# A linear-attention and maxout kernel: nine tokens per partition for k and v, 64-row pairs on TensorE, and q's maxima applied to the numerators

## The chip, the cores and the metric

The kernel runs on one core of one Trainium2 chip. A core has five engines that are used here: TensorE (PE, its weight loads are shown apart as PEld), VectorE (DVE), ScalarE (ACT), GpSimd (POOL) and SyncE (SP), which issues most of the transfers. Times are device microseconds (us) of the whole program; lower is better. The kernel before takes 297.06 us, the median of three runs (296.61 to 297.08).

## The reference

Sixty-four attention heads (8 batches of 8), 576 tokens each, 64 channels. Each head is a linear attention with a feature map phi, and what comes out goes through a feed-forward layer with a maximum over three projections:

```python
def phi(x):                                   # x: q or k, (b, h, 576, 64)
    proj = einsum('bhsd,df->bhsf', x, w_phi)  # 128 features
    proj = proj - max(abs(proj), axis=-1, keepdims=True)
    return concatenate([exp(proj), exp(-proj)], axis=-1)
q_p, k_p = phi(q), phi(k)
kv  = einsum('bhsf,bhsd->bhfd', k_p, v)       # sum over tokens
z   = sum(k_p, axis=2)
num = einsum('bhsf,bhfd->bhsd', q_p, kv)
den = einsum('bhsf,bhf->bhs', q_p, z)[..., None] + 1e-06
x   = num / den                               # to (4608, 512)
h   = maximum(maximum(x @ w1, x @ w2), x @ w3)
out = h @ w_out
```

With m the row maximum and p the projection, the first half of phi is exp(p - m) and the second exp(-(p - m)), so a token's factor is exp(-m) on the one and exp(m) on the other. For k both factors can be put on v. For q a common factor of both halves cancels in num / den, and what is left is exp(-2m) on the first half alone.

## The kernel before

**Tiling.** A unit is 4 heads of one batch; 16 units make the 64 heads, units 2b and 2b+1 make batch b. A unit's 4 × 576 tokens stand in 18 tiles of 128 tokens: 16 "main" tiles (4 per head, a partition holds 4 consecutive tokens of a head) and 2 tail tiles (the last 64 tokens of two heads each, one head in partitions 0 to 63, the other in 64 to 127). The same layout holds for q, k and v, so each of them is loaded by one main transfer (rows of 1,024 bytes) and two tail transfers (rows of 256 bytes).

**One unit's steps** (function `attention`):
- T: q and k are turned into `qkT` (q's channels in rows 0 to 63, k's in rows 64 to 127), by 36 TensorE transposes for units 0 to 3 (line 517), by a transfer that transposes (line 530) for the others.
- G: projections of both with `w2` into PSUM tiles `psq` and `psk`: per main tile two matmuls that use 64 rows each (line 557), per tail tile one of 128 rows and 256 columns (line 552).
- Ek: two exponentials of each group of k's projections on ACT (line 570); maxima of |projection| for q and k on DVE (line 576).
- em, vab, vtl: the factors exp(-m), exp(m) of k (line 613), times v on POOL (lines 618 and 633).
- M: q's projections again, with features on partitions, minus q's maxima. For units 0 to 3 the maxima are subtracted by further matmuls with `minus`, the negated identity (lines 655 and 657: 18 products of 128 columns per unit). For the others the maxima are transposed (pmT, line 584), copied (line 588) and put by a transfer (line 592) into row 64 of `qkT`, which k's channels no longer need, and one matmul with `wphi_m` (row 64 holds -1) does both (line 653).
- Eq: two exponentials of each group (line 665).
- K: key features times values, 18 matmuls of 128 rows per pair of heads (lines 682 and 685), copied to `kv_sb` (line 689).
- N: numerators and denominators, 10 matmuls of 65 columns per head into one PSUM tile (line 703); DVE takes a reciprocal and multiplies (lines 709 and 710) into `x_sb`.
- X: `x_sb` transposed into `xT`, on TensorE and a copy (lines 723 and 726) for units 0 to 5, by a transfer (line 733) for the others.

**Feed-forward.** Function `chunk` runs nine times: for each batch its tokens 0 to 511, and last for the 64 tail tokens of all 8 batches (512 again). It does 54 + 54 up projections in all, each of 4 matmuls of 512 columns (line 756), the maxima (lines 762, 764, 766), and the down projections (lines 784 and 789), copied out (line 797) and stored. Before the first chunk, differences of the weights (line 831), a transposed w1 (lines 843 and 846) and its product with w_out (lines 857 and 861) are made.

**Order.** Nothing is scheduled at run time. The string `PLAN` is an order table written out by hand or by a planner: 1,542 words, each a node's number, its engine, the slots of its buffers and a planned start. `plan` sorts nothing: the nodes are emitted in the order of the words, and each engine executes its own in that order, waiting by semaphores for what it needs. All PSUM tiles share 8 banks. `fill` adds matmuls on a constant tile `idle` (line 889, called idlers) where the table leaves TensorE free for long, from the planned end of the node that sets `idle` (node 2, `2D0@0.5`) on.

## Time and profile before

| what | value |
|---|---|
| median of three runs | 297.06 us (296.61 to 297.08) |
| span of the profiled execution, first to last instruction | 295.1 us |
| mean granted TensorE clock in it | 0.998 |
| DVE busy | 214.3 us (73%) |
| ACT busy | 196.3 us (67%) |
| POOL busy | 138.1 us (47%) |
| instructions on PE | 2,973 matmuls, 3,015 weight loads |

The profile gives no device time of the profiled execution beside its span; the span is 1.96 us (297.06 - 295.1) shorter than the median of the runs, which is what lies around it (launch and end).

How to read it: a row of groups gives line, engine, operation, output<-input, shape, count, then busy time, mean ns of one, idle time before and what ended it. A row of the timeline gives start and length in us, then engine and operation. Matmuls are pipelined, so a matmul's length (about 380 ns for 512 columns) is longer than the distance to the next one (about 216 ns); costs on a busy engine are therefore read as distances from start to start. A row of windows gives a stretch, its length, and for each engine the busy time in it with the number of instructions, then the granted clock, the busy share of the transfers' engines and GB/s.

### The profile page before, as it was taken

To read this page: it belongs to the slowest core of one execution; us is meant where nothing else is said; L and a number is where in the kernel's file an instruction comes from. 1 tells how busy PE (TensorE), PEld (TensorE's weight loads), DVE (VectorE), ACT (ScalarE), POOL (GpSimd) and SP (SyncE) were. 2 spreads that over 40 slices of the span, in tenths; PEclk is the share of its full clock that TensorE was granted. 3 is DMA by queue.
4 is the path that set the end of the run, shared out by engine and by line. 5 is a ranking of instruction groups with operands and counts; after the bars stand their busy time and mean duration, and the time that the engine had idled before them with its cause. 6 is when DMAs were issued, how large, how long until landed. Compare 5 with 4: busy or idle time off the path is not lost.

```text
span 295.1 us, 7535 instructions
## 1 busy us (share of the span) xinstructions
PE 281.6 (95%) x2973; PEld 161.5 (55%) x3015; DVE 214.3 (73%) x453; ACT 196.3 (67%) x457; POOL 138.1 (47%) x172
## 2 busy tenths in 40 slices
PE   8699999999999999999999999999999999999994
PEld 3356676556556556556556555655555564444442
DVE  5793798987878988888879776889697365061541
ACT  2499888587878599979879788867954870300300
POOL 4487995672773464943982369009072500000000
PEclk9999999999999999999999999999999999999999
DMA  6999998799379979997979779935392034300306
GB/s 134 190 196 224 229 221 286 167 234 226 99 182 328 209 203 318 230 230 167 285 165 189 220 204 244 189 102 117 90 209 64 2 83 116 142 2 0 142 8 134
DMA packets 87879, 50.02 MB, mean 170 GB/s; under 512 B 56100, under 2 KB 83364, under 8 KB 87844
## 3 DMA queue, kind: packets, MB, share of 16 engines
q1 hardware_dynamic: 81684, 44.50, 61.2%
q0 software_dynamic: 6080, 4.98, 11.0%
q8 instruction: 23, 0.38, 0.5%
q14 instruction: 12, 0.10, 0.1%
q10 hardware_dynamic: 80, 0.07, 0.1%
HBM read 34.67 MB, written 9.44 MB: 149 GB/s over the span
## 4 chain that ended last, share of the span: by engine, by line
PE 79%; DVE 9%; ACT 4%; POOL 3%; DMA 2%; issue 2%; POOLq 0%; ACTq 0%; DVEq 0%
PE ups L756 27%; PE ops L789 15%; PE ops L784 11%; PE psn L703 6%; PE kvps L682 5%; PE psq L557 4%; PE psm L653 4%; DVE mk L576 2%; DMA qk_bf<-in_q_dram 2%; ACT Ek L570 2%; DVE mqp L576 2%; DVE x_sb L710 1%; POOL vab L618 1%; PE pxT L723 1%; DVE w_bf L831 1%
## 5 line engine op out<-in xcount | busy, mean ns | idle before, releaser
L756 PE MATMUL ups<-xT,w_bf 128*128 128x512 bf16 x412 | 100.4, 379 | 2.2 <-DVE mqp L576 0.8
L665 ACT ACTIVATE Eq<-psm 128x512 bf16<-128x512 f32 (+1 forms) x160 | 79.6, 579 | 8.8 <-PE psm L653 7.3
L570 ACT ACTIVATE Ek<-psk 128x512 bf16<-128x512 f32 x128 | 70.8, 607 | 16.1 <-DVE mk L576 8.7
L618 POOL TENSOR_TENSOR vab<-v_raw,em 128x1024 bf16<-128x1024 f32 (+1 forms) x36 | 61.6, 1715 | 21.2 <-ACT em L613 20.1
L756 PEld LDWEIGHTS <-w_bf 128*128 128x128 bf16 x432 | 40.7, 98 | 45.3 <-issue 1.0
L576 DVE TENSOR_REDUCE mqp<-psq 128x4 bf16<-128x512 f32 (+1 forms) x80 | 47.7, 629 | 7.5 <-PE psk L557 4.4
L789 PE MATMUL ops<-wout_bf,hT 128*128 128x512 bf16 (+1 forms) x211 | 49.5, 373 | 0.6 <-issue 0.2
L762 DVE TENSOR_TENSOR hT<-hT,ups 128x512 bf16<-128x512 bf16 x54 | 36.0, 683 | 17.4 <-PE ups L756 9.1
L576 DVE TENSOR_REDUCE mk<-psk 128x4 f32<-128x512 f32 x64 | 42.2, 680 | 1.1 <-PE psk L557 0.7
L710 DVE TENSOR_TENSOR x_sb<-psn,rden 128x320 bf16<-128x320 f32 x64 | 31.5, 492 | 2.2
L789 PEld LDWEIGHTS <-hT 128*128 128x128 bf16 x222 | 21.1, 98 | 21.7
L797 ACT COPY osb<-ops 128x512 f32<-128x512 f32 (+1 forms) x20 | 11.5, 581 | 31.3 <-PE ops L789 23.6
L764 ACT ACTIVATE hT<-ups 128x512 bf16<-128x512 f32 x27 | 16.4, 617 | 21.5 <-PE ups L756 21.5
L703 PEld LDWEIGHTS <-Eq 128*128 128x128 bf16 x640 | 24.6, 97 | 6.8
L703 PE MATMUL psn<-kv_sb,Eq 128*128 128x65 bf16 x640 | 26.1, 194 | 0.1
L633 POOL TENSOR_TENSOR vtl<-v_raw,em 64x256 bf16<-64x256 f32 x32 | 19.7, 615 | 13.2 <-ACT em L613 10.2
L766 DVE TENSOR_SCALAR hT<-ups 128x512 bf16<-128x512 f32 x27 | 18.1, 683 | 10.6 <-PE ups L756 10.6
L784 PE MATMUL ops<-xT 128*128 128x512 bf16 x89 | 24.1, 379 | 0.4
L682 PEld LDWEIGHTS <-Ek 128*128 128x128 bf16 x512 | 21.6, 98 | 4.5 <-DVE mqp L576 0.5
L682 PE MATMUL kvps<-vab,Ek 128*128 128x65 bf16 x512 | 22.8, 194 | 0.5 <-DVE mqp L576 0.2
L504 POOL CAST qk_bf<-q_raw 128x128 bf16<-128x128 f32 (+2 forms) x22 | 16.8, 773 | 11.6 <-DMA q_raw<-in_q_dram 11.3
L797 DVE COPY osb<-ops 128x512 f32<-128x512 f32 (+1 forms) x17 | 11.4, 671 | 13.7 <-PE ops L789 13.6
(80 smaller groups left out, 333.5 us busy)
## 6 DMA issues: line engine op xcount, KB each, us to landing
v_raw<-in_v_dram SPq DMA_DIRECT2D x16, 512.0 KB, 6.8
out_dram<-osb SPq DMA_DIRECT2D x32, 256.0 KB, 2.9
k_raw<-in_k_dram SPq DMA_DIRECT2D x12, 512.0 KB, 5.6
q_raw<-in_q_dram SPq DMA_DIRECT2D x12, 512.0 KB
w_bf<-in_moe_w_dram POOLq DMA_DIRECT2D x3, 768.0 KB, 8.3
k_raw<-in_k_dram SPq DMA_DIRECT2D x16, 64.0 KB, 4.5
q_raw<-in_q_dram SPq DMA_DIRECT2D x16, 64.0 KB, 6.4
v_raw<-in_v_dram SPq DMA_DIRECT2D x16, 64.0 KB, 4.3
```

The costliest lines, as they stand in the source:

```text
L570: nc.scalar.activation(Ek[s]()[:, t0:t0 + n, :], of(1), EXP, scale=1.0 - 2.0 * s)
L576: nc.vector.tensor_reduce((mq, mk)[c]()[:, t0:t0 + n], of(c), AXX, ALU.max, apply_absolute_value=True)
L618: (nc.vector if n_.eng == "DVE" else nc.gpsimd).tensor_tensor(vab()[:, g, t0:t1, 0:D], raw_part(u, 2, t0, t1), em()[:, g, t0:t1].unsqueeze ...
L665: nc.scalar.activation(Eqb()[s][:, cols], psm()[:, 0:n * P], EXP, scale=1.0 - 2.0 * s)
L682: nc.tensor.matmul(kvps()[:, ab, g, :], lhsT=Ek[g]()[:, t, :], rhs=vab()[:, g, t, :], start=(g + ab + c == 0), stop=False)
L703: nc.tensor.matmul(psn()[:, c, :], lhsT=Eqb()[g][:, t0:t0 + P], rhs=kv()[:, pr, ab, g, :], start=(g == 0), stop=(g == 1))
L710: nc.vector.tensor_tensor(x_sb()[:, pr, :, ab, :], psn()[:, :, 0:D], rden().to_broadcast([P, 5, D]), ALU.mult)
L756: nc.tensor.matmul(ups(), lhsT=w_bf[i + 1][:, ct, j * P:(j + 1) * P], rhs=tokens_of(ct), start=(ct == 0), stop=(ct == CT - 1))
L762: nc.vector.tensor_tensor(hT()[:, j, :], hT()[:, j, :], ups(), ALU.max)
L784: nc.tensor.matmul(ops_()[:, 0:width], lhsT=tile_of(ct, tt), rhs=line_w[c_i > MOVE][:, ct, cols], start=(ct == 0), stop=False)
L789: nc.tensor.matmul(ops_()[:, 0:width], lhsT=hT()[:, j, tt * P:(tt + 1) * P], rhs=wout_bf[:, j, cols], start=False, stop=(j == JT - 1))
L797: copy_on[n_.eng](part()[:, 0:width], ops_()[:, 0:width])
```

## The change

What the changed program does otherwise:

1. **k and v: nine tokens per partition.** Two heads' 1,152 tokens are taken as one list, and each partition holds 9 consecutive ones: 64 partitions per head. One transfer (rows of 2,304 bytes) brings what three brought; k and v have no tail tiles. q keeps its layout.
2. **K as 64-row pairs.** Head ab of a pair lies in partitions 64·ab to 64·ab + 63. K is 36 matmuls of 64 rows per pair of heads, alternating between the two row halves and two PSUM tiles; units 2 to 15 do both pairs in one node. `vtl` and its instructions are gone; `vab` has 18 tiles.
3. **Transposed q as 64-row pairs.** In tiles 0 to 7 q lies in rows 0 to 63 of `qkT` and k in rows 64 to 127, in tiles 8 to 17 the other way round. M takes tiles t and t + 8 together, one in each half, with the plain weights `wph` (both halves hold w_phi). G does all 18 tiles as 64-row pairs.
4. **q's maxima on the numerators.** M no longer subtracts them: `minus`, the products of line 657, pmT, mT, the transfer of line 592, `w2`, `wphi_m`, `mqp` and their memsets are gone. N puts the two halves of phi into two PSUM tiles; ACT makes `sq` = exp(-2m) (2 small instructions per unit); DVE multiplies the first accumulator by it into `y` in SBUF, adds the second, takes one reciprocal per pair of heads, and the product with it goes to POOL (22 of 32) or DVE (10 of 32).
5. **The rest.** The copy to `xT` is 640 columns wide; POOL moves the second head's tail before it copies tails for the last chunk; `x_last` shares a slot with `q_raw`; DVE reduces k before q in each group.
6. **New order table**, 1,572 words. The node that sets `idle` is now node 1 and stands late (`1D@32.5`); the program that results has no idlers. On ACT and DVE, 36 instead of 27 of the first maxima (`hT`, a ReLU) go to ACT, and all three copies of the transposed w1.

The diff, cut to its core (`any_of` sets a node's function and lets the table choose the engine; `copy_on` is the copy of that engine):

```diff
+EARLY = 2
+PT = UT // 2
 PLAN = """
-9S0@0.7 4S@1.3 11S@2.5 13S@3.1 8S0@4.4 15S0@5.6 14S@6.9 6G0@0.5 0G@1.4 1G@2.1 7G@2.6 90G1@3.4 17G@9.3 91G@9.6 12A@6.8
...
+    def rows_of(what, u, p0, p1):
+        src, h0 = (q, k, v)[what], (u % 2) * HU
+        return src[u // 2, h0 + 2 * p0:h0 + 2 * p1].rearrange("h s d -> (h s) d").rearrange(
+            "(pr i j) d -> i pr (j d)", i=P, j=PT)
...
+        if what:
+            t0 = (u % 2) * UT
+            eng.dma_start(dst[:, t0:t0 + UT, :].rearrange("p (r j) d -> p r (j d)", j=PT), rows_of(what, u, 0, 2))
+            return
...
+    def side(t):
+        return int(t >= MT // 2)
...
-    n_minus = node("const", 0, {"POOL": 0.5}, lambda: nc.gpsimd.tensor_scalar_mul(minus, ident, -1.0), [n_ident], [])
-    n_const = node("const", 0, {"DVE": 2.2}, zeros, [n_idle], [])
...
                         for c in range(2):
-                            nc.tensor.transpose(tps()[c * D:(c + 1) * D, n, :], qk()[:, c, t0 + n, :], ident)
+                            r = (c + side(t0)) % 2 * D
+                            nc.tensor.transpose(tps()[r:r + D, n, :], qk()[:, c, t0 + n, :], ident)
...
-                        if n == 2:
-                            nc.tensor.matmul(psq()[:, 2 * i:2 * i + 2, :].rearrange("p a f -> p (a f)"), lhsT=cols,
-                                             rhs=w2.rearrange("p a f -> p (a f)"), start=True, stop=True)
-                            continue
                         for c, ps in enumerate((psq, psk)):
-                            nc.tensor.matmul(ps()[:, i, :], lhsT=cols[r, :], rhs=w2[r, c, :], start=True, stop=True)
+                            r0 = (c + side(t0)) % 2 * D
+                            nc.tensor.matmul(ps()[:, i, :], lhsT=cols[r0:r0 + D, :], rhs=wph[r0:r0 + D, :], start=True, stop=True)
...
-                for i in range(n):
-                    nc.tensor.matmul(psm()[:, i * P:(i + 1) * P], lhsT=mq()[:, t0 + i:t0 + i + 1].to_broadcast([P, P]),
-                                     rhs=minus, start=False, stop=(i == n - 1))
...
+                for pr in prs:
+                    for g in range(2):
+                        for j in range(PT):
+                            for ab in range(2):
+                                r, t = slice(ab * D, (ab + 1) * D), PT * pr + j
+                                nc.tensor.matmul(kvps[ab]()[:, pr, g, :], lhsT=Ek[g]()[r, t, :], rhs=vab()[r, g, t, :],
+                                                 start=(pr == prs[0] and g + j == 0), stop=(pr == prs[-1] and g == 1 and j == PT - 1))
...
+        for parts in ([(0, 4), (8, 4)], [(4, 4), (12, 4)], [(16, 2)]):
+                for (t0, n), psm in zip(parts, psms):
+                    r0 = side(t0) * D
+                    nc.tensor.matmul(psm()[:, 0:n * P], lhsT=wph[r0:r0 + D, :], rhs=qkT()[r0:r0 + D, t0 * P:(t0 + n) * P],
+                                     start=True, stop=True)
...
+            nc.scalar.activation(sq()[:, :, 0:4], mq()[:, 0:MT].rearrange("p (h c) -> p h c", c=4), EXP, scale=-2.0)
+            nc.scalar.activation(sq().rearrange("p (r ab) c -> p r ab c", ab=2)[:, :, :, 4],
+                                 mq()[:, MT:UT].unsqueeze(2).to_broadcast([P, 2, 2]), EXP, scale=-2.0)
...
-                            nc.tensor.matmul(psn()[:, c, :], lhsT=Eqb()[g][:, t0:t0 + P],
-                                             rhs=kv()[:, pr, ab, g, :], start=(g == 0), stop=(g == 1))
+                            nc.tensor.matmul(psn[g]()[:, c, :], lhsT=Eq[g]()[:, t0:t0 + P], rhs=kv()[:, pr, ab, g, :],
+                                             start=True, stop=True)
...
-                    nc.vector.reciprocal(rden(), psn()[:, :, D:W])
-                    nc.vector.tensor_tensor(x_sb()[:, pr, :, ab, :], psn()[:, :, 0:D], rden().to_broadcast([P, 5, D]),
-                                            ALU.mult)
+                n_ = nd("xu", {"DVE": 0.42}, lambda pr=pr, ab=ab, psn=psn, y=y: nc.vector.tensor_tensor(
+                    y()[:, ab], psn[0](), sq()[:, 2 * pr + ab, :].unsqueeze(2).to_broadcast([P, 5, W]), ALU.mult),
+                sums.append(nd("xw", {"DVE": 0.42}, lambda ab=ab, psn=psn, y=y: nc.vector.tensor_tensor(
+                    y()[:, ab], y()[:, ab], psn[1](), ALU.add), [n_], [psn[1], y], locks=[psn[1]]))
+            n_ = nd("xr", {"DVE": 0.22}, lambda y=y, rden=rden: nc.vector.reciprocal(rden(), y()[:, :, :, D:W]), sums, [y, rden])
+            n_ = nd("x", {"POOL": 1.42, "DVE": 0.74}, None, [n_], [y, rden, x_sb])
```

More of the change, by code (lines that the diff above doesn't have):

```diff
@@ L544, in attention @@
             for t0, n in part:
-                psq, psk = bank("psq", [P, 4, DF]), bank("psk", [P, 4, DF]) if n == 4 else None
+                psq, psk = bank("psq", [P, 4, DF]), bank("psk", [P, 4, DF])
                 given.append((t0, n, psq, psk))
@@ L611, in emf @@
+        for t0, t1, of, need in ranges:
             def emf(t0=t0, t1=t1):
@@ L695, in attention @@
-        for pr in range(2):
+            y = buf("y", 2, [P, 2, 5, W], FP32)
+            rden = buf("rden", 2, [P, 2, 5, 1], FP32)
+            sums = []
             for ab in range(2):
-                psn = bank("psn", [P, 5, W])
+                psn = [bank("psn", [P, 5, W]) for _ in range(2)]
                 def nmm(pr=pr, ab=ab, psn=psn):
                     for c in range(5):
-                        t0 = (8 * pr + 4 * ab + c if c < 4 else MT + pr) * P + (D if c == 4 and ab else 0)
+                        t0 = (8 * pr + 4 * ab + c if c < 4 else MT + pr) * P
```

662 lines of the change are left out of this document (291 added, 371 removed).

## The prediction

> **What bounds the kernel now.** I read the chain that ended last, then busy time by stage, then the starts of single instructions. Stages: up to the first up projection (46.2 us), to the last attention work on TensorE (245), to the last matmul (291), to the end.
>
> ```profile
> span 295.1 us, 7535 instructions
> PE 79%; DVE 9%; ACT 4%; POOL 3%; DMA 2%; issue 2%; POOLq 0%; ACTq 0%; DVEq 0%
> ```
> ```profile
> 0.00:46.20 46.20, 40.74 (x570) 25.24 (x574) 33.59 (x83) 34.45 (x82) 35.24 (x53) 1.00 1.09 205
> 46.20:245.00 198.80, 195.39 (x2189) 114.78 (x2223) 162.40 (x342) 155.15 (x364) 102.48 (x119) 1.00 0.76 184
> 245.00:291.00 46.00, 45.50 (x219) 21.46 (x220) 18.32 (x30) 6.57 (x12) 0.40 (x1) 1.00 0.25 77
> 291.00:295.10 4.10, 0.00 (x0) 0.00 (x0) 0.00 (x0) 0.12 (x1) 0.00 (x0) 0.86 0.54 118
> ```
> ```profile
> 12.00:46.20 34.20, 31.73 (x485) 21.34 (x489) 26.93 (x62) 31.77 (x79) 30.16 (x40) 1.00 1.17 220
> 100.00:120.00 20.00, 19.79 (x214) 11.20 (x213) 18.10 (x35) 17.32 (x42) 10.00 (x13) 1.00 0.97 261
> ```
>
> From 46.2 to 291 TensorE is the bound: busy 240.9 of 244.8 us, and the chain is 79% PE. What is saved there is saved from the end. DVE is next, 162.4 of 198.8 in the second stage (82%), at best 18.1 of 20 (90.5%). Up to 46.2 PE's busy time is padded with idlers, and the fullest engine is ACT: 31.77 of the 34.2 us after 12 (93%).
>
> **Prices on TensorE.** Distances from start to start, since rows overlap.
>
> ```profile
> 63.57 0.22 PE L557 MATMUL psq<-w,qkT 64*128 64x128 bf16 x1
> 63.57 0.22 PE L557 MATMUL psk<-w,qkT 64*128 64x128 bf16 x1
> 63.63 0.22 PE L557 MATMUL psq<-w,qkT 64*128 64x128 bf16 x1
> 63.63 0.22 PE L557 MATMUL psk<-w,qkT 64*128 64x128 bf16 x1
> 63.78 0.39 PE L552 MATMUL psq<-w,qkT 128*128 128x256 bf16 x2
> ```
> ```profile
> 86.68 0.42 PE L682 MATMUL kvps<-vab,Ek 128*128 128x65 bf16 x8
> 86.94 0.22 PE L685 MATMUL kvps<-vtl,Ek 128*128 128x130 bf16 x1
> 87.00 0.42 PE L682 MATMUL kvps<-vab,Ek 128*128 128x65 bf16 x8
> 87.95 0.38 PE L653 MATMUL psm<-qkT,wphi_m 128*128 128x512 bf16 x1
> 88.17 1.03 PE L756 MATMUL ups<-xT,w_bf 128*128 128x512 bf16 x4
> ```
> ```profile
> 111.83 0.22 PE L584 MATMUL pmT<-ident,mqp 128*128 128x128 bf16 x1
> 111.88 0.27 PE L653 MATMUL psm<-qkT,wphi_m 128*128 128x256 bf16 x1
> 111.99 0.42 PE L682 MATMUL kvps<-vab,Ek 128*128 128x65 bf16 x8
> 60.87 0.39 PE L657 MATMUL psm<-minus,mqp 128*128 128x128 bf16 x4
> 9.15 0.64 PE L517 MATMUL tps<-ident,qk_bf 128*64 128x128 bf16 x16 [1.43 <-DMA qk_bf<-in_q_dram]
> ```
>
> Two 64-row matmuls on different halves start at the same time, and the next pair follows 0.056 later: they run side by side. A 65-column matmul costs 0.26/8 = 0.0325, a 130-column one 0.06, 512 columns 0.216 (0.22 in the row), 256 columns 0.11, a product of line 657 (0.39 - 0.22)/3 = 0.056, pmT 0.05, a transpose (0.64 - 0.22)/15 = 0.028. Going from a pair to full rows takes 63.78 - 63.63 = 0.15 where 0.056 is the pair's own: 0.095 for the switch. The way in costs the same:
>
> ```profile
> 9.72 0.23 PE L557 MATMUL psq<-w,qkT 64*128 64x128 bf16 x1
> ```
>
> The last of the transposes before it starts at 9.15 + 0.64 - 0.22 = 9.57, this pair 0.15 later.
>
> **TensorE after the first up projection.** Counts are those of the two instruction orders behind the first line-756 matmul, by these prices:
> - G: 200 pairs and 24 of 256 columns (13.8 us) become 234 pairs (13.0): -0.8.
> - M: 52 of 512 columns, 13 of 256, 18 products, 12 pmT (11.2 + 1.4 + 1.0 + 0.6 = 14.3) become 27 pairs of 512 columns and 13 of 256. A 512-column pair is not in the trace; between 0.216 (side by side) and 0.43 I take 0.22, by the pairs of line 557: 7.3. So -7.0.
> - K: 448 of 65 columns and 56 of 130 (14.6 + 3.4 = 17.9) become 504 pairs of 65 columns. Such a pair is not in the trace either. From below 0.0325, the single matmul of that width; from above 0.056, the pair of 128 columns. The loads of a line-557 pair start together too, and its 0.056 is that of a single 128-column matmul, so width sets the price: I take 0.034, 17.1. So -0.8 (-1.5 to +10.3).
> - T: the 16 transposes that were behind the first up projection now stand ahead: -0.4. N, X and the feed-forward keep their counts.
> - Switches: 50 become 88, by 0.095: +3.6.
>
> Sum -5.4. The trace weighs the pairs' price by starts; the Trainium skill, "TensorE: Matmul & The Clock Gate", section "Wait — 56ns, not 53.3ns?", has a floor of about 25 ns from start to start however narrow a matmul is. If that held for each matmul of a pair, 504 pairs would cost at least 25.2 us and the sum would be +2.7; the simultaneous starts above speak against it.
>
> **DVE behind the same point.** It is the cover that may go.
>
> ```profile
> 60.83 0.19 DVE L709 RECIPROCAL rden<-psn 128x5 f32<-128x5 f32 x1
> 61.05 0.49 DVE L710 TENSOR_TENSOR x_sb<-psn,rden 128x320 bf16<-128x320 f32 x1
> 61.46 0.18 DVE L709 RECIPROCAL rden<-psn 128x5 f32<-128x5 f32 x1
> ```
> ```profile
> L762 DVE TENSOR_TENSOR hT<-hT,ups 128x512 bf16<-128x512 bf16 x54 | 36.0, 683 | 17.4 <-PE ups L756 9.1
> L766 DVE TENSOR_SCALAR hT<-ups 128x512 bf16<-128x512 f32 x27 | 18.1, 683 | 10.6 <-PE ups L756 10.6
> ```
>
> A reciprocal costs 0.22, the product of 320 elements 0.41. Now 56 heads (units 2 to 15) cost 56 × 0.63 = 35.3. After: two products of 325 (0.415 each, one operand from PSUM as now), 0.22 per pair of heads, and eight products of 640 from SBUF (no such row; 0.41 at the width of 320, 0.82 at twice, I take 0.74): 46.5 + 6.2 + 5.9 = 58.6, +23.3. Five reductions move behind the first up projection (+3.0); nine maxima (0.61 each, 683 ns less an overlap of 0.07) and three output copies go to ACT (-7.3); mT goes (-1.6); fewer, wider kv copies (-2.7); `xT` and weight differences +2. Together +16.7: 162.4 becomes 179, in a stage of 198.8 - 5.4 = 193.4: 93%, more than the best 20 us now. TensorE stays the longer, but the queues get tight; PE's idle time there, 3.4 us now, I raise by 0.9. POOL has room: 102.5 of 198.8, minus `vtl` (-17), plus 22 products of 640 (1.3 each from line 618's 1,907 ns for 1,024 and 1,042 for 512), which N's results now wait for. Stage two and three: -5.4 + 0.9 = -4.5.
>
> ```profile
> L618 POOL TENSOR_TENSOR vab<-v_raw,em 128x1024 bf16<-128x1024 f32 x28 | 53.4, 1907 | 19.6 <-ACT em L613 18.4
> L618 POOL TENSOR_TENSOR vab<-v_raw,em 128x512 bf16<-128x512 f32 x8 | 8.2, 1042 | 1.7 <-ACT em L613 1.6
> ```
>
> **The start.** ACT, the fullest engine, starts late:
>
> ```profile
> 7.76 0.69 DVE L576 TENSOR_REDUCE mqp<-psq 128x4 bf16<-128x512 f32 x1 [0.60 <-PE psk L557]
> 9.83 0.69 DVE L520 COPY qkT<-tps 128x1024 bf16<-128x1024 bf16 x1 [1.38 <-PE tps L517]
> 10.44 0.68 DVE L576 TENSOR_REDUCE mk<-psk 128x4 f32<-128x512 f32 x1
> 11.22 1.57 ACT L570 ACTIVATE Ek<-psk 128x512 bf16<-128x512 f32 x3 [4.02 <-PE psk L557]
> ```
>
> The first Ek reads the bank that DVE's mk reads, and starts when mk has ended (10.44 + 0.68); mk stands behind q's reduction and a copy that waits for the second half of q. The new order has mk first: it can end at 7.76 + 0.68, and Ek start near 8.4, 2.8 earlier. ACT's work ahead of the first up projection falls: 31 Ek and 27 Eq become 25 and 24 (0.5 each from 1.57 for three, less for the narrow ones: -5.0), two more copies of the transposed w1 (1.0 each), +0.5 for a fourth product copy, `sq` +0.4, less for em, kv and vd (-0.9): -3.0. DVE's falls by about 4 (reductions, memsets, w1 copies less; x more), so it does not take over: 33.6 - 4 from 6.5 on ends at 36.
>
> The idlers go, and they ran ahead of everything:
>
> ```profile
> 1.87 0.15 PEld L889 LDWEIGHTS <-idle 128*128 128x128 bf16 x1 [0.28 <-issue]
> 2.30 0.15 PEld L889 LDWEIGHTS <-idle 128*128 128x128 bf16 x1 [0.28 <-issue]
> 3.91 0.96 PEld L889 LDWEIGHTS <-idle 128*128 128x128 bf16 x5 [0.18 <-issue]
> ```
>
> They follow each other by 0.43 at first and by about 0.2 from 3.9 on: the array starts at half speed. Without them the first T and G run so: one T (0.45) and one G (0.23) doubled, +0.7. First up projection: 46.2 - 2.8 - 3.0 + 0.7 = 41.1.
>
> **Sum.** 297.06 - 5.1 - 4.5 = **287.5 us** (span 285.5, and 1.96 around it as now).
>
> **Rivals.**
> 1. *Narrow pairs don't overlap* (slower). In K the two halves take turns, in 0.056 a pair: 504 × (0.056 - 0.034) = +10.9, 298.4. From 0.053 a pair on it decides against the change. For it: four instructions per pair in 0.034 would be more than any row shows. Against it: the line-557 starts.
> 2. *DVE becomes the bound.* Held to its best share now, 90.5%, 179 us of work need 197.8 instead of 194.3: +3.5, 291.0. For it: 93% asked. Against it: PE still has more work.
> 3. *The start gains nothing*, since transfers set it (their engines' share is 1.17 after 12 us): first up at 46.2, 292.6. Against it: k and v move in longer rows, and ACT's late start is no transfer's doing.
> 4. *The array stays at half speed through the start.* Its 21 us of work ahead of the first up projection would take 42 and, with 24 switches (2.3) and a begin at 5.8, end at 50: 296.4. The Trainium skill, "TensorE: Matmul & The Clock Gate", section "What's actually happening", has the clock full after about 3.4 us of sustained work and halved after an idle window; no row here shows it falling back. Against it: from 14 us on PE is too busy for that.
> 5. *M's 512-column pairs take turns* (the pairs are no pairs): 27 × 0.21 = +5.7, 293.2.
>
> **How the numbers follow.** Forecast 0.60, rivals 0.12, 0.13, 0.08, 0.03, 0.02, other 0.02. Lower end: the start as early as DVE allows (36.3, -4.8), pairs at 0.0325 (-0.8), no new idle time (-0.9): 281. Upper end: rival 1, 298.5. The forecast's own range is 282 to 292. A difference under 0.2% (296.5 to 297.7) can't be told from none. Slower 0.16 (most of rival 1, and 2 with 3 or 5 together), the same 0.05, faster 0.79.
>
> **What would show it.** First up projection near 41; K's matmuls 0.017 apart on average; 0.095 at 113 switches in place of 78; DVE over 90% between the first up projection and the last attention work; Ek's first start near 8.4 to 9. Wrong would be: K bursts of 36 longer than 0.8, PE idle time over 6 us behind the first up projection, or that projection behind 46.

## The result, and the profile after

Before 297.07 us, after **293.07 us** (medians; 292.23 to 293.61): ratio 0.987, 95% interval 0.984 to 0.990. The forecast was 287.5. The direction holds, the size is 4.0 us instead of 9.6, and the time lies 1.1 us outside the forecast's own range (282 to 292). The profiled execution took 292.23 us with a span of 290.1.

The page after, its span and its chain that ended last by engine:

```profile
span 290.1 us, 8572 instructions
PE 74%; DMA 15%; DVE 6%; issue 1%; POOL 1%; SPq 1%; DVEq 0%; POOLq 0%
```

TensorE's share of the chain fell from 79% to 74%, and DMA's went from 2% to 15%. The windows by stage (busy time and number of instructions of PE, its loads, DVE, ACT, POOL; granted clock, DMA share, GB/s):

```profile
0.00:42.70 42.70, 31.41 (x557) 21.99 (x557) 31.67 (x73) 33.04 (x78) 27.85 (x43) 0.96 1.09 230
42.70:240.20 197.50, 193.19 (x2722) 107.66 (x2723) 178.97 (x355) 165.04 (x404) 126.48 (x117) 1.00 0.74 185
240.20:286.20 46.00, 45.98 (x229) 21.65 (x225) 19.10 (x32) 6.57 (x12) 3.38 (x5) 1.00 0.23 67
```

First up projection at 42.8 (before 46.3), last attention work at 240.2 (244.7), last matmul at 286.2 (290.7). So the start gained 3.5 us and everything behind it 0.95. DVE's work is what the forecast said, 179 us. The waits of TensorE behind the first up projection (us in total, times, the longest), first of the kernel before, then after:

```profile
PE ups L756 <- DVE mqp L576: 0.8, 2, 0.4
PE ups L756 <- DVE w_bf L831: 0.4, 1, 0.4
```
```profile
PE ups L688 <- DVE w_bf L763: 1.4, 1, 1.4
PE ups L688 <- DVE mq L548: 0.9, 1, 0.9
PE ups L688 <- DMA xT<-x_sb: 0.9, 1, 0.9
PE ups L688 <- POOL w_bf L763: 0.9, 2, 0.7
PE psn L638 <- DVE kv_sb L593: 0.3, 1, 0.3
PE psn L638 <- DVE y L641: 0.3, 1, 0.3
```

The kernel before has two more, of 0.2 us each. Waits for DVE's maxima (`mqp`, now `mq`) and for the weights' differences were there before; the weights' have grown, and those for a transfer into `xT` and for N's operands are new. They stand at few places. The timeline of the changed kernel, PE's rows at them:

```profile
42.79 1.90 PE L688 MATMUL ups<-xT,w_bf 128*128 128x512 bf16 x8 [0.71 <-POOL w_bf L763]
44.87 1.90 PE L688 MATMUL ups<-xT,w_bf 128*128 128x512 bf16 x8 [0.18 <-POOL w_bf L763]
48.16 1.90 PE L688 MATMUL ups<-xT,w_bf 128*128 128x512 bf16 x8 [1.39 <-DVE w_bf L763]
52.85 3.68 PE L688 MATMUL ups<-xT,w_bf 128*128 128x512 bf16 x16 [0.90 <-DVE mq L548]
136.61 1.24 PE L688 MATMUL ups<-xT,w_bf 128*128 128x512 bf16 x5 [0.89 <-DMA xT<-x_sb]
```

I measure lost time from start to start: eight matmuls from 44.87 on need 8 × 0.216 = 1.73, so the next could start at 46.60 and does at 48.16: 1.56 lost. Summed that way over everything behind the first up projection, TensorE loses 6.4 us, 3.2 of them up to 55 us, 1.05 at 135, 1.2 at 194 to 197; in the kernel before it was about 2.0 (places where a record is missing left out). What is left is work: 243.4 - 6.4 = 237.0 after, 244.4 - 2.0 = 242.4 before, **5.4 less, as forecast**.

The windows alone would hide this. By their busy time TensorE's idle time in the second stage went from 3.4 us (198.8 - 195.4) to 4.3 (197.5 - 193.2), just the forecast's +0.9. That agreement is luck: a matmul behind a wait is counted busy for its whole 0.38 us, where the next start is only 0.216 away, and more than half of the 3.4 us before are places where a record is missing.

Where the early waits come from is in POOL's and DVE's rows and in the chain:

```profile
40.62 4.20 POOL L763 TENSOR_TENSOR w_bf<-w_bf 128x1024 bf16<-128x1024 bf16 x2 [3.42 <-DMA w_bf<-in_moe_w_dram]
```
```profile
47.05 1.05 DVE L763 TENSOR_TENSOR w_bf<-w_bf 128x1024 bf16<-128x1024 bf16 x1 [2.52 <-DMA w_bf<-in_moe_w_dram]
```
```profile
16.17 30.79 DMA w_bf<-in_moe_w_dram
47.05 1.05 DVE w_bf L763
```

The second weight lands at 40.5, the third at 47.0, 30.8 us behind its issue; the differences that the up projections multiply come right behind. In the kernel before the third landed at 43.4. The median from issue to landing of the three weights went from 8.3 us to 25.1:

```profile
w_bf<-in_moe_w_dram POOLq DMA_DIRECT2D x3, 768.0 KB, 8.3
```
```profile
w_bf<-in_moe_w_dram POOLq DMA_DIRECT2D x3, 768.0 KB, 25.1
```

The two medians are not like for like. Before, the three loads were issued at 12.4, 26.0 and 33.8 us; now all three are issued between 13.9 and 16.2 on one queue, and each also waits for those ahead of it. What tells is the last landing: 3.6 us later than before, though its load was issued 17.7 us earlier.

What runs beside them in the changed kernel are SP's loads of k and q for the units 4 and 5, about 2.2 MB:

```profile
13.91 0.40 SPq L373 DMA_DIRECT2D k_raw<-in_k_dram  x1
18.63 1.31 SPq L383 DMA_DIRECT2D q_raw<-in_q_dram  x2
19.99 0.60 SPq L378 DMA_DIRECT2D q_raw<-in_q_dram  x1
20.64 0.51 SPq L373 DMA_DIRECT2D k_raw<-in_k_dram  x1
21.18 0.82 SPq L378 DMA_DIRECT2D q_raw<-in_q_dram  x1
```

In the kernel before, the loads for these units are issued from 34.5 us on.

**Theory:** TensorE's saving came as forecast; it was given back where the new order lets the weights land late, and at a few late waits. **Rivals:** VectorE, now 91% busy, is the bound; the array, cold without idlers, holds the start; K's narrow pairs or M's wide ones are dearer than they look.

### The profile page after: what moved, and what is told of

It reads as the page before. It is cut to its first block, busy times and chain, and to the rows that moved or that the text cites. A ratio compares the mean times of both kernels' runs of the same rounds, so it can differ in the third digit from the quotient of the medians.

```text
span 290.1 us, 8572 instructions
## 1 busy us (share of the span) xinstructions
PE 270.6 (93%) x3502; PEld 151.3 (52%) x3502; DVE 230.2 (79%) x458; ACT 204.7 (71%) x493; POOL 157.7 (54%) x163
## 4 chain that ended last, share of the span: by engine, by line
PE 74%; DMA 15%; DVE 6%; issue 1%; POOL 1%; SPq 1%; DVEq 0%; POOLq 0%
PE ups L688 31%; PE ops L721 14%; DMA w_bf<-in_moe_w_dram 11%; PE ops L716 10%; PE psn L638 6%; PE kvps L587 5%; PE psq L536 4%; PE psm L607 3%; DMA q_raw<-in_q_dram 2%; DMA xT<-x_sb 2%; DVE w_bf L763 1%; DVE x_sb L648 1%; DVE y L644 1%; PE pxT L658 1%; PE psk L536 1%
## 5 line engine op out<-in xcount | busy, mean ns | idle before, releaser
L545 ACT ACTIVATE Ek<-psk 128x512 bf16<-128x512 f32 (+1 forms) x160 | 83.6, 572 | 12.9 <-PE psk L536 6.7
L566 POOL TENSOR_TENSOR vab<-v_raw,em 128x1152 bf16<-128x1152 f32 (+1 forms) x36 | 69.5, 1950 | 35.8 <-ACT em L558 35.8
L548 DVE TENSOR_REDUCE mk<-psk 128x4 f32<-128x512 f32 (+1 forms) x80 | 48.7, 630 | 4.7 <-PE psk L536 3.2
L548 DVE TENSOR_REDUCE mq<-psq 128x4 f32<-128x512 f32 (+1 forms) x80 | 48.6, 628 | 2.3 <-PE psk L536 1.3
L648 POOL TENSOR_TENSOR x_sb<-y,rden 128x640 bf16<-128x640 f32 x22 | 27.4, 1253 | 21.9 <-DVE rden L646 21.0
L641 DVE TENSOR_TENSOR y<-psn,sq 128x325 f32<-128x325 f32 x64 | 29.5, 488 | 6.9 <-PE psn L638 5.0
L644 DVE TENSOR_TENSOR y<-y,psn 128x325 f32<-128x325 f32 x64 | 29.4, 488 | 1.4
L536 PE MATMUL psq<-wph,qkT 64*128 64x128 bf16 x288 | 25.9, 224 | 1.2 <-DVE qkT L500 1.0
L536 PEld LDWEIGHTS <-qkT 64*128 64x128 bf16 x576 | 18.6, 97 | 15.8 <-issue 12.0
L536 PE MATMUL psk<-wph,qkT 64*128 64x128 bf16 x288 | 25.4, 224 | 0.3 <-DVE v_raw L479 0.3
L587 PE MATMUL kvps<-vab,Ek 64*128 64x65 bf16 x1152 | 22.7, 193 | 0.3 <-ACT Eq L613 0.2
## 6 DMA issues: line engine op xcount, KB each, us to landing
w_bf<-in_moe_w_dram POOLq DMA_DIRECT2D x3, 768.0 KB, 25.1
```

The source lines that it names most:

```text
L536: nc.tensor.matmul(ps()[:, i, :], lhsT=cols[r0:r0 + D, :], rhs=wph[r0:r0 + D, :], start=True, stop=True)
L545: "ek", {"ACT": 0.485 if n == 4 else 0.28}, lambda s=s, t0=t0, n=n, psk=psk: nc.scalar.activation(Ek[s]()[:, t0:t0 + n, :], psk()[:, 0:n, ...
L548: reds.append(nd(kind, {"DVE": 0.607 if n == 4 else 0.34}, lambda ps=ps, m=m, t0=t0, n=n: nc.vector.tensor_reduce(m()[:, t0:t0 + n], ps()[ ...
L566: made.append(any_of(n_, lambda n_, g=g, t0=t0, t1=t1: (nc.vector if n_.eng == "DVE" else nc.gpsimd).tensor_tensor(vab()[:, g, t0:t1, 0:D] ...
L587: nc.tensor.matmul(kvps[ab]()[:, pr, g, :], lhsT=Ek[g]()[r, t, :], rhs=vab()[r, g, t, :], start=(pr == prs[0] and g + j == 0), stop=(pr == ...
L644: sums.append(nd("xw", {"DVE": 0.42}, lambda ab=ab, psn=psn, y=y: nc.vector.tensor_tensor(y()[:, ab], y()[:, ab], psn[1](), ALU.add), [n_] ...
```

## Experiments

Ratios are to the kernel before, with 95% intervals. "Last matmul" is that of the profiled execution; between two executions of one kernel it differed by 1.4 us (experiments 7 and 14) and by 2.3 (the changed kernel and experiment 9), so differences under that are read from medians and from the waits.

**1. No load of the second and third weight.**

```diff
+        nc.vector.memset(w_bf[1], 0.01)
+        nc.vector.memset(w_bf[2], 0.01)
         nc.sync.dma_start(wphi_f[0:D, :], w_phi)
...
+        if i in (1, 2):
+            return
         dst = (w_bf + [wout_bf])[i]
```

> The changed kernel, without the loads of the second and third weight: two constants written by DVE at the very start stand in for them, and all later work on them is done. Theory (the weights' transfers hold the first up projections): the difference of the weights no longer waits for a landing at 40.6 and 47.0; the first up projection comes right behind the last copy of xT (41.4 us in the changed kernel), at 41.5 to 42, the 3.2 us of TensorE's idle time up to 55 go, and the kernel takes 288.5 to 290 us. Rival (the attention of the first two units sets the start, the waits for weights would only be replaced): first up projection at 42.5 or later, at least 2 us of idle time stay up to 55, 292 us or more.

289.81 us (0.976, 0.971 to 0.980). The lost time up to 55 us, behind the first up projection, fell from 3.2 to 0.55 us, but that projection came at 43.8, later than with the loads. Half of each side was right: the idle time went, as the theory has it, and the projection came late, as the rival has it. The stand-in was not free: the two constants cost DVE 2.62 us each at the very start, so experiments 5 and 6 do without them.

**2. Without the second accumulator's addition on DVE.**

```diff
-                sums.append(nd("xw", {"DVE": 0.42}, lambda ab=ab, psn=psn, y=y: nc.vector.tensor_tensor(
-                    y()[:, ab], y()[:, ab], psn[1](), ALU.add), [n_], [psn[1], y], locks=[psn[1]]))
+                sums.append(nd("xw", {"DVE": 0.42}, lambda: None, [n_], [psn[1], y], locks=[psn[1]]))
```

> The changed kernel without the addition of the second accumulator on VectorE (64 instructions of 325 elements, 0.41 us each: 26 us of VectorE's work left out; the output holds only the first accumulator's part). Theory: VectorE is late in a few places only; TensorE's idle time between 120 and 200 us (2.5 us) goes, that before 55 us stays, since weights are waited for there: 290 to 291.5 us. Rival (VectorE is the bound of the whole stage): the idle time before 55 us goes too, and the kernel takes 289 us or less. A third outcome, 292.5 us or more: neither, the late idle time has another cause.

291.65 us (0.984, 0.977 to 0.990), last matmul at 285.9. DVE lost 20 us of work in the stage,

```profile
42.40:240.00 197.60, 192.77 (x2724) 107.32 (x2725) 158.63 (x301) 165.23 (x405) 126.50 (x116) 1.00 0.73 185
```

and the stage kept its 197.6 us. The median is 1.4 us under the changed kernel's, in overlapping intervals; in the two profiles the last matmul moved by 0.3 us for 20 us less work. VectorE's amount of work is not the bound: rival 2 of the prediction is out. But my theory's half is out as well. The late waits stayed:

```profile
136.74 1.02 PE L683 MATMUL ups<-xT,w_bf 128*128 128x512 bf16 x4 [1.52 <-DMA xT<-x_sb]
194.59 0.87 PE L634 MATMUL psn<-kv_sb,Eq 128*128 128x65 bf16 x21 [0.32 <-DVE kv_sb L589]
```

By what ends them they hang on a transfer and on a short chain (kv product, its copy, the product that reads it), not on a late queue.

**3. K's two halves in turn.**

```diff
-                for pr in prs:
-                    for g in range(2):
-                        for j in range(PT):
-                            for ab in range(2):
+                for ab in range(2):
+                    for pr in prs:
+                        for g in range(2):
+                            for j in range(PT):
```

> The changed kernel with the matmuls of the kv product in another order: all of the first half's 64 rows, then all of the second's, the same matmuls on the same operands. Theory (the two halves of a 65-column pair run side by side, 0.033 us a pair): out of the pairs each matmul costs 0.031 to 0.033 by itself, 0.064 a pair; 504 pairs behind the first up projection lose 16 us, 307 to 310 us in all. Rival (narrow pairs take turns, and K is cheap for another reason): 292.5 to 294 us.

305.82 us (1.030, 1.024 to 1.035), last matmul at 299.7, 13.5 later. The same 72 matmuls in the chain of the changed kernel and of this one:

```profile
57.08 1.15 PE kvps L587 x72
```
```profile
68.60 2.20 PE kvps L583 x72
```

A pair takes 1.15/36 = 0.032, out of the pairs 0.061. Narrow pairs run fully side by side: rival 1 is out, and K's term (0.034 a pair) was right. The loss in all, 12.8 us, stayed under the 16 expected; what took up the rest I did not look for.

**4. Idlers back in the changed kernel** (the node that sets `idle` first).

```diff
-1189T21@31.2
+1189T2@31.2
-1D@32.5
+1D1@0.3
```

> The changed kernel with the idle matmuls of the kernel before put into TensorE's gaps up to the first up projection, so that the array does not start cold. Theory (the start is set by transfers and by ACT, not by TensorE): the pairs are 0.056 apart from 6 us on instead of 0.105, the first up projection stays at 42.3 to 42.9, and the kernel takes 292.3 to 293.3 us. Rival (the cold array costs the 1.6 us by which the first up projection missed the forecast): first up projection at 41.5 or earlier, 291.5 us or less.

292.29 us (0.985, 0.980 to 0.990), first up projection at 43.0, last matmul at 286.15. Nothing that can be told. But the idlers did not keep the array fast either, so this is no test of a fast array. Thirty-six transposes (T) that start near 15 us, in the kernel before, the changed kernel, and with idlers:

```profile
15.35 1.20 PE L517 MATMUL tps<-ident,qk_bf 128*64 128x128 bf16 x36
```
```profile
14.46 2.25 PE L495 MATMUL tps<-ident,qk_bf 128*64 128x128 bf16 x36 [0.49 <-DVE mq L548]
```
```profile
14.28 2.25 PE L492 MATMUL tps<-ident,qk_bf 128*64 128x128 bf16 x36 [0.49 <-DVE mq L545]
```

They take 1.20 us at full speed and 2.25, half speed, in both later kernels. Without idlers the array is slow up to about 17 us; with them it is fast from about 6 us on, and slow again from 12.5 to 22.8. The pairs were 0.056 apart only for a while, not from 6 us on as I expected.

**5 and 6. One weight for both operands of the differences**, without and with idlers; the up projections multiply zeros.

```diff
+        if i in (1, 2):
+            return
         dst = (w_bf + [wout_bf])[i]
...
-                (nc.vector if n_.eng == "DVE" else nc.gpsimd).tensor_tensor(dst[:, :, c], dst[:, :, c], w_bf[0][:, :, c],
+                (nc.vector if n_.eng == "DVE" else nc.gpsimd).tensor_tensor(dst[:, :, c], w_bf[0][:, :, c], w_bf[0][:, :, c],
```

> The changed kernel, without the loads of the second and third weight and without any instruction in their place: the differences of the weights take the first weight for both operands, so that the up projections multiply zeros; all other work stays. Unlike the run with constants, nothing is added to VectorE's start. Theory (the weights' transfers hold the first up projections): first up projection at 41.5 to 42.3 us, TensorE's idle time from there to 55 us under 0.7 us instead of 3.2, last matmul at 282.3 to 283.3 us (286.2 in the changed kernel), 289 to 290.3 us. Rival (the attention of the first two units sets the start): first up projection at 42.7 or later, last matmul at 284 us or later.

> As the run with one weight, and with the idle matmuls of the kernel before in TensorE's gaps up to the first up projection. Theory (the cold array costs little, because ACT and VectorE set the start): within 0.7 us of the run with one weight. Rival (with the weights out of the way the cold array is what is left of the missed 1.7 us): first up projection at least 1 us earlier than in the run with one weight, 1 us less in all.

290.67 us (0.978, 0.971 to 0.985) and 289.60 (0.975, 0.970 to 0.981). The waits for weights are gone (0.6 us lost up to 55), yet the first up projection came at 44.4 and the last matmul at 285.15: in 5 the rival's numbers came, not the theory's. DVE's rows show why:

```profile
35.81 0.81 DVE L646 TENSOR_TENSOR x_sb<-y,rden 128x640 bf16<-128x640 f32 x1
39.39 2.20 DVE L646 TENSOR_TENSOR x_sb<-y,rden 128x640 bf16<-128x640 f32 x1
```
```profile
37.17 3.74 POOL L761 TENSOR_TENSOR w_bf<-w_bf 128x1024 bf16<-128x1024 bf16 x2
```

The same product of two SBUF operands takes 0.81 us once and 2.20 the other time. The second started while POOL was at two differences of the weights, which end at 37.17 + 3.74 = 40.91: 1.52 us later, and 2.20 - 1.52 = 0.68. It looks as if DVE had waited for them to end and then taken 0.68. With weights that come early, POOL's differences meet the products of unit 1's x on DVE, the last step ahead of xT. With the idlers (first up projection at 43.8, last matmul at 284.0) the time is 1.1 us less, within the two intervals: neither side is shown.

**7 and 14. The loads of units 4 and 5 later.** The changed kernel, complete; the words of the order table that move (k and q of the two units on SP; on POOL their casts, which now stand behind the weights' differences):

```diff
-401S0@12.2 329S0@15.6 400S@18.8 328S@22.9 327S@26.0
+401S0@34.21 329S0@34.22 400S@34.23 328S@34.24 327S@34.25
-406G1@26.6 404G@29.0 403G@29.5 405G@30.1 334G2@30.7 407G@38.8 408S1@39.6
+406G1@39.51 404G@39.52 403G@39.53 405G@39.54 407G@39.55 408S1@39.65 334G2@39.7
```

> The changed kernel, complete, with another order of SP's and POOL's work ahead of 45 us: the loads of k and q of the units 4 and 5 (2.2 MB, issued from 13.9 to 21.2 us in the changed kernel) come behind the two loads of v at 34.3, and their casts on POOL behind the three differences of the weights. Theory (these loads take the DMA engines from the weights): the last weight lands by 41 us instead of 47.0, TensorE's idle time from the first up projection to 55 us is 1.2 us or less instead of 3.2, first up projection at 41.5 to 42.5, 290 to 291.5 us. Rival (the weights' own queue has a pace that no other load changes): last landing at 45 us or later, 292.5 to 294 us. A second rival: the weights land early, but the products of unit 5 at 59 us wait for the later data, and the gain is given back there.

> The kernel with the later loads once more, as the measure for the run beside it: 289.2 to 290 us.

**289.58 us** (0.976, 0.971 to 0.981), and 289.98 (0.978, 0.974 to 0.981) when run again. The weights take 18.6 us in the median and 21.4 at most; the third lands at 37.7 instead of 47.0 (37.3 in the second run). POOL's three differences now run in one piece from 34.2, and the up projections without a break:

```profile
34.16 7.45 POOL L760 TENSOR_TENSOR w_bf<-w_bf 128x1024 bf16<-128x1024 bf16 x3 [1.43 <-DMA w_bf<-in_moe_w_dram]
```
```profile
42.41 5.35 PE L685 MATMUL ups<-xT,w_bf 128*128 128x512 bf16 x24
48.46 4.49 PE L685 MATMUL ups<-xT,w_bf 128*128 128x512 bf16 x20
```

Last matmul at 283.4 instead of 286.2, from the order of five loads and their casts. The queues between 25 and 34 us tell the theory from its rival: q0 is the weights' queue, q1 SP's (packets, MB, time of the packets as a share), in the changed kernel and in this one:

```profile
q0 software_dynamic: 1015, 1.13, 72.1%
q1 hardware_dynamic: 1021, 1.06, 42.5%
```
```profile
q0 software_dynamic: 1380, 1.85, 116.3%
```

With nothing on SP's queue the weights' queue moves 1.85 MB in these 9 us instead of 1.13. The rival (a pace of the weights' queue that no load changes) is out, and the later data are not missed at 59 us: TensorE's one new wait is 0.61 us at 54, for POOL. This settles the main cause. The Trainium skill, "DMA: Bandwidth & Descriptors", section "Queues, rings and completion order", has each DMA engine take turns between the queues that have work for it; the landings, 25.1 us beside SP's loads and 18.6 without, agree.

In the second run's profile the lost time up to 55 us is low again (0.5), but the first up projection came at 44.0 and the last matmul at 284.85. The same table met the hazard of experiment 5 at a worse moment: the first of the two products of x started just behind a difference on POOL.

```profile
36.02 2.55 DVE L645 TENSOR_TENSOR x_sb<-y,rden 128x640 bf16<-128x640 f32 x1
```

So the first up projection did not come earlier for certain: 42.4 and 44.0 here, 42.8 and 45.5 in the two profiles of the changed kernel.

**8. M on 128 rows**, the second step of the forecast undone (`wq` holds the weights for each half, with zeros in the other 64 rows).

```diff
-nc.tensor.matmul(psm()[:, 0:n * P], lhsT=wph[r0:r0 + D, :], rhs=qkT()[r0:r0 + D, t0 * P:(t0 + n) * P],
+nc.tensor.matmul(psm()[:, 0:n * P], lhsT=wq[:, side(t0), :], rhs=qkT()[:, t0 * P:(t0 + n) * P],
```

> The changed kernel with the products of the transposed q (M) on 128 rows instead of pairs of 64, the factor padded with zeros: the second step of the forecast undone, the rest kept. Theory (512-column pairs run side by side, 0.22 us a pair): 27 pairs and 13 narrower matmuls cost 13.1 us instead of 7.4 behind the first up projection, 78 switches instead of 88 give 1.0 back: +4.7, last matmul at 290 to 291.3 us, 296.8 to 298.3 us. Rival (M's matmuls are not on the path, since others are waited for): less than +2 us.

295.50 us (0.995, 0.993 to 0.998; 296.8 to 298.3 expected), last matmul at 289.0. The 512-column pair is as forecast: two in the time of one in the changed kernel, one behind the other here.

```profile
28.57 0.39 PE L607 MATMUL psm<-qkT,wph 64*128 64x512 bf16 x2
```
```profile
70.14 0.59 PE L610 MATMUL psm<-qkT,wq 128*128 128x512 bf16 x2
```

But only 2.8 us came of the 4.7 that the prices give: the lost time fell from 6.4 to 4.7 us, since the transfer at 135 and the products at 156 found TensorE later than they were (read from the waits). Work saved on TensorE is partly turned into waits for work that does not get faster with it.

**9 to 13. What is left.** 9 is the changed kernel once more; 10 has the later loads with idlers; 11 has later loads, and swaps engines: unit 1's two products of x on POOL, the second weight's differences on DVE, three casts of unit 4 behind POOL's v products; 12 is 11 with idlers; 13 is 11 with DVE's third difference ahead of two other instructions.

```diff
-163D1@31.4 171D@33.3 1179G@34.6 1178G@36.7 1177G@39.5 331G@41.6 333G@42.2 334G2@39.7
+163G1@31.4 171G@33.3 1179D@34.6 1178D@36.7 1177D@39.5 334G2@47.71 331G@47.72 333G@47.73
...
-1180D@42.8
+1180D@40.95
```

> The changed kernel itself once more, as the measure for the runs beside it: 292 to 293.6 us, last matmul at 286 to 286.5 us.

> The kernel with the later loads, and with the idle matmuls in TensorE's gaps up to the first up projection. With the weights' wait gone, the cold array is now nearer to the path than in the run with idle matmuls alone, which gained nothing that could be told. Theory (the cold array costs 0.5 to 1.2 us of the start, as between the two runs with one weight): last matmul 0.5 to 1.2 us ahead of the run with the later loads (283.4), 288.3 to 289.2 us. Rival (the start is set by VectorE and ACT alone): no difference, 289.3 to 290 us.

> The kernel with the later loads, and in it three more moves: the two products that make unit 1's x go from VectorE to POOL, the three differences of the second weight from POOL to VectorE, and three casts of unit 4's q and k behind unit 2's v products on POOL. In the run with the later loads VectorE's two products took 1.44 and 1.81 us beside POOL's differences, where the same product takes 0.82 with POOL idle. Theory (the two engines slow each other down when both work on two operands in SBUF, and this sets the last copy of xT): POOL's two products at 1.25 us each end by 38.7 instead of 39.6, differences of 0.7 to 1.1 us on VectorE, first up projection at 41 to 41.9 instead of 42.4, the wait of 0.77 us at 54 us gone: 288 to 289 us. Rival (VectorE is full there: 29.2 of 30.8 us, the differences come late on it): first up projection at 42.4 or later, 289.5 us or more.

> Both: later loads, swapped engines, idle matmuls. If both theories hold, the gains add: last matmul at 281.3 to 282.5 us, 287.3 to 288.6 us. If the start has one chain after another with little between them, no more than 0.3 us below the better of the two.

> The kernel with the swapped engines, and VectorE's third difference of the third weight right behind its second, ahead of an activation of hT and a maximum, so that it is done before POOL's v products start. Theory (the two engines slow each other down, 2.3 us in place of 0.67): that difference takes 0.65 to 1.1 us, the wait of 2.0 us at 48 to 50 us falls below 0.6, last matmul 1.4 to 2 us ahead of the run with swapped engines (284.2), 287.3 to 288.4 us. Rival (the wait is VectorE's amount of work: 18.9 of 19.1 us from 41 to 60): the wait stays within 0.5 us, 289 us or more.

| run | us | ratio, 95% | first up | last matmul |
|---|---|---|---|---|
| 9 changed again | 293.02 | 0.986 (0.983 to 0.990) | 45.5 | 288.5 |
| 10 later, idlers | 290.27 | 0.978 (0.975 to 0.980) | 42.8 | 284.9 |
| 11 swapped | 289.51 | 0.974 (0.971 to 0.977) | 40.95 | 284.2 |
| 12 swapped, idlers | 289.77 | 0.977 (0.974 to 0.980) | 42.1 | 285.9 |
| 13 difference ahead | **288.78** | 0.975 (0.971 to 0.979) | 40.9 | 282.7 |

The medians of 10 to 13 all lie above what the theories expected, by 0.4 to 1.2 us. Idlers gained nothing that can be told in 10 and 12, but neither run had a fast array (the granted clock was half from 11.5 to 21.7 us in 10, from 10.6 to 17.4 in 12), and 10 has a new wait of 2 us at 51 that is not the idlers' own (below). What the cold array costs thus stays open. That it can cost something 9 suggests: the granted clock fell to half for 3.4 us at 36, while the products `pm` (transposed w1 times w_out) ran, and the first up projection came 2.7 us later than in the first profile of this kernel (0.9 of it was there at the first Ek already); the profiled execution was 1.6 us over the median. Swapping the engines brought the first up projection to 40.95, where the forecast had it (41.1), but a wait of 2 us appeared behind it. It stands behind DVE's third difference of the third weight, which met POOL's v products: that difference and the two v products in 11; the same difference in 10, where it starts 0.13 us behind a v product; and the second and third difference in 13, ahead of the v products:

```profile
47.36 2.33 DVE L760 TENSOR_TENSOR w_bf<-w_bf 128x1024 bf16<-128x1024 bf16 x1
```
```profile
47.02 4.64 POOL L563 TENSOR_TENSOR vab<-v_raw,em 128x1152 bf16<-128x1152 f32 x2
```
```profile
48.55 2.54 DVE L760 TENSOR_TENSOR w_bf<-w_bf 128x1024 bf16<-128x1024 bf16 x1
```
```profile
45.55 1.85 DVE L760 TENSOR_TENSOR w_bf<-w_bf 128x1024 bf16<-128x1024 bf16 x2
```

One difference in 2.33 or 2.54 us, or two in 1.85. In 13 the wait of 2 us fell to 0.3, as expected, but two others of 0.7 came ahead of it, at 44 and 47: 1.7 us lost between 44 and 50 instead of 2.5. Last matmul 1.5 us earlier, while the median fell only by 0.7, short of what I expected. Its interval and that of the plain later loads overlap: that 13 is the faster of the two is not shown. Both are faster than the changed kernel.

**15. Plain copies in place of the ten transposing DMAs into xT** (the up projections of these units then multiply untransposed data).

```diff
-                nc.sync.dma_start_transpose(
-                    out=xT[:, b, ct0:ct0 + 2, :].rearrange("p q (t c) -> p (q t) c", c=P),
-                    in_=x_sb().rearrange("p q t a d -> p (q t a d)"))
+                nc.sync.dma_start(xT[:, b, ct0:ct0 + 2, :].rearrange("p q (t c) -> p (q t) c", c=P),
+                                  x_sb().rearrange("p q t a d -> p (q t) (a d)"))
```

> The changed kernel with plain DMA copies in place of the ten transposing ones that bring x into xT (the up projections of these units then multiply untransposed data). Theory (the wait of 1.05 us at 135 us is the time of that DMA, 4.9 us from issue to landing in the changed kernel): the copy lands within 3.5 us, the wait is below 0.3 us, last matmul at 284.8 to 285.4 us, 291.7 to 292.4 us. Rival (x itself is late, whatever carries it): the wait stays at 0.7 us or more.

291.79 us (0.983, 0.980 to 0.986), last matmul at 284.85, and no wait at 135. The transfer that was waited for takes 4.9 us from issue to landing in the changed kernel and 3.6 here: the wait was the transposing DMA's own time. The kernel before has the same ten; they came in time there, behind a slower TensorE.

## Why the prediction was right and wrong

- **TensorE's work: right.** Forecast -5.4, measured -5.4. K 0.032 a pair (forecast 0.034), M side by side, and the switches 0.095 each way: in the changed kernel's timeline the last pair at 133.28 is followed by full rows at 133.43, 0.15 later, where 0.056 is the pair's own. G's pairs took 0.058 in the mean (0.056), which about makes up for K's.
- **DVE's work: right in amount (179 us), wrong as a danger.** That it agrees to the microsecond is partly luck: the reciprocals took 0.16 instead of 0.22, the products of x more than their price. DVE was 91% busy, and 20 us less of its work changed the stage by nothing. The products of x, priced 0.74, take 0.82 to 1.35 in the changed kernel and up to 2.55 where they meet POOL's differences (14).
- **Ek's first start: right**, 8.24 (forecast 8.4).
- **The step that failed: the weights' landing, priced at nothing, in the start and behind it.** "First up projection: 46.2 - 2.8 - 3.0 + 0.7 = 41.1" put the gain on ACT, and the third rival, that transfers set the start, got 0.08 with "ACT's late start is no transfer's doing". ACT did start earlier, and `xT` was done near 41.4; but an up projection needs the weights' differences too. The new order moves the loads of the units 4 and 5 some 20 us ahead, into the weights' transfer. The first up projection waits 0.7 us for a difference (the row at 42.79), and some 2.1 us are lost to weights behind it (the third one and DVE's late differences; 1.1 of the 3.2 up to 55 had its like before). Together 2.8, which is what the last matmul gains in experiment 7; by the medians the five loads behind the weights bring 3.0 to 3.5.
- **The rest of the start, 0.9 us: ACT's early start was not carried through.** ACT's four Ek from 8.24 on are followed by a wait that the kernel before does not have:

```profile
12.42 0.60 ACT L545 ACTIVATE Ek<-psk 128x512 bf16<-128x512 f32 x1 [2.12 <-PE psk L536]
11.38 0.42 PE L495 MATMUL tps<-ident,qk_bf 128*64 128x128 bf16 x4 [2.22 <-POOL qk_bf L487]
11.04 0.53 POOL L487 CAST qk_bf<-q_raw 128x128 bf16<-128x128 f32 x2 [4.63 <-DMA q_raw<-in_q_dram]
```

  ACT waits for G's next projections, TensorE ahead of them for a cast of q's tail tiles, and POOL for their transfer, issued at 3.75 and landed at 10.9. In the kernel before a load of these tiles lands at 11.5 too, but ACT has only begun there. So a transfer does hold ACT, only not its first instruction; with idlers, in experiment 4, TensorE waits 2.81 us at this place, so it is not the cold array. No experiment parts this from ACT's work, which fell by 1.4 us in the windows (34.45 to 33.04), not 3.0.
- **Idle time further on.** "PE's idle time there, 3.4 us now, I raise by 0.9": as lost time it went from 2.0 to 6.4, by 4.4. Beside the 2.1 for weights these are 1.05 for the transfer at 135 (experiment 15) and some 1.2 for the chain of kv product, copy and product at 194. The last is read from the waits only; I did not try to part it.
- **The cold array: priced too short, its cost open.** The forecast has half speed for the first T and G alone, and rival 4 has it to the end of the start, "from 14 us on PE is too busy for that" against it. The transposes at 14.46 still ran at half speed, and so did the stretch from 20.8 to 24.2. It did not last to the end as rival 4 has it. "No row here shows it falling back" is wrong: the prediction's own window from 291.0 to 295.1 has a granted clock of 0.86. No run of the changed kernel or of its variants kept the array fast up to the first up projection.
- **A sum.** Rival 1's 504 × (0.056 - 0.034) is 11.1, not 10.9; its time would be 298.6.

Ledger, in the profiled executions to the last matmul: start -3.5 (forecast -5.1), work -5.4 (-5.4), idle time +4.4 (+0.9): -4.5 (-9.6).

## What to carry to other kernels

When a change comes with a new order, list the transfers by issue time in both and ask of each which one it now runs beside: five loads moved ahead on a free queue cost 3 us, by holding up those that were awaited. Work taken off the bound engine is kept only as far as what it waits for gets earlier too. And a two-operand instruction of VectorE on SBUF data should not be planned behind a long one of GpSimd where either is on the path.

## What the runs showed of the hardware

- DVE's instructions with two SBUF operands waited for the POOL instruction in progress, whole. DVE's two products of unit 1's x in experiment 7, and POOL's second and third difference (the first starts at 34.16, in the row shown there):

```profile
35.53 1.44 DVE L645 TENSOR_TENSOR x_sb<-y,rden 128x640 bf16<-128x640 f32 x1
37.82 1.81 DVE L645 TENSOR_TENSOR x_sb<-y,rden 128x640 bf16<-128x640 f32 x1
```
```profile
36.25 5.36 POOL L760 TENSOR_TENSOR w_bf<-w_bf 128x1024 bf16<-128x1024 bf16 x2
```

  By the trace the first difference ends 0.76 us behind the first product's start, the second 1.12 us behind the second's; 0.68 is left of each product, as in experiment 5, and 0.69 (2.55 - 1.86) in 14. Where the product comes first it takes 0.82. The weights' difference on DVE took 0.68 with POOL idle and 0.54 plus the rest of POOL's instruction otherwise (1.41 with 0.86 to go in the changed kernel). The Trainium skill, "SBUF — State Buffer", section "Who interferes with whom", has a VectorE instruction with two SBUF inputs contend with a GpSimd one that reads SBUF, for a shared pair of ports under an exclusive lock; the trace agrees. The prediction left it out.
- Two 64-row matmuls of 65 columns on different halves, each with its own load, went through at 0.032 us a pair. The Trainium skill, "TensorE: Matmul & The Clock Gate", section "Wait — 56ns, not 53.3ns?", which I weighed in the prediction, would have it at twice its floor of about 25 ns if that held for each; it does not hold across the halves.
- The granted clock fell back to half, for 3.4 us or up to three times that, ahead of 55 us in six of the profiled executions: in all four with idlers (4, 6, 10, 12), and in two of the twelve without (the first one of the changed kernel, and 9). In the 3.4 us ahead of each of these eight stretches TensorE was busy for 26% to 74% of the time; in 9, 46%. No run tests where the border lies.
